# First pair's rotary steps on VectorE, and TensorE given turns and products ahead of the first scores, in a fused attention and gated feed-forward kernel

## The chip, the cores and the metric

The kernel runs on one core of a Trainium2 chip. The time is the device time of one execution, in microseconds (us). Of the kernel before, three runs are shown: 659.55 us in the median, 659.51 the lowest and 661.09 the highest. The engines are PE (TensorE, matmul), DVE (VectorE), ACT (ScalarE), POOL (GpSimd) and SP (SyncE, which issues most DMAs). Each works through its own list of instructions in order, and an instruction waits on semaphores for what other engines and DMAs have to finish first.

## The reference, cut to what matters

```
def rotate(x):                       # rotary position embedding, x: 8 x 8 heads x 576 x 64
    x1, x2 = (x[..., :half], x[..., half:])
    return np.concatenate([x1 * cos - x2 * sin, x1 * sin + x2 * cos], axis=-1)
scores = scale * np.matmul(rotate(q), rotate(k).transpose(0, 1, 3, 2))
attn = softmax(scores)               # max subtracted, exp, divided by the sum
x = np.matmul(attn, v)               # then heads side by side: 8 x 576 x 512
gate = sigmoid(causal 5-tap convolution of x along the positions, per channel)
out = ((gate * (x @ w_val)) @ w_out)
```

## The kernel before, in words

The 64 heads are worked off as 32 pairs, two heads on the 128 partitions. For each pair, q and k come in as [128, 2, 576]: the values, and the values with the two halves of the head swapped. The rotary step multiplies the first by the cosine table, the second by the sine table (`rope_mul`, L211, twice), adds them (`rope_add`, L215), rounds the sum to the fast matmul format on ACT (`qk_hi`, L222), and takes the rest of that rounding (`qk_lo`, L226). The scores are sums of three products of these high and low parts (`s_mm`, L254), in five chunks: four of 128 queries for both heads, c0 to c3, and a mixed one, c4, for the last 64 queries of both heads. A chunk of one head is a 576-wide tile in PSUM; there are three such buffers. DVE takes the row maximum (`s_max`, L260, called max0 to max8), ACT the exponential (`s_exp`, L273). The probabilities are turned on PE (`t_mm`, L302 and L315) or by DVE and DMAs (L288), multiplied with v (L358, L368, L373, L376), normed, convolved, and pass through the two weight matrices (L454).

One of the two heads reads its keys in a rotated order: its first 64 key columns are a copy of the last 64 (`k_front`, L189 on the tile k). So both heads' scores need the end of the keys first, and the copy needs the later key half.

The first pair's q and k come in two parts each, so that work can start early. Key halves are columns 0 to 287 and 288 to 575; the query parts are columns 0 to 255 and 256 to 575. The tables come in the same two halves on ACT's DMA queue, and ACT scales each (`scale_tab`, L207) before it is used. The keys of the plan end in `_0` and `_1` for the earlier and later part: `kmul0_0`, `kmul1_0`, `kadd_0`, `khi_0`, `klo_0` are the steps of the earlier key half.

The weight matrices w_val and w_out are stored as 64-bit floats. Each is loaded in four pieces of 512 KB and decoded on DVE and ACT in six steps, L488, L490, L491, L493, L494, L495, then split into a high and a low part with PE's help (L525 to L532). The decode of the first pieces of w_val stands between the first pair's maxima.

A planner sets the order: each step is a job with a due time, its base time plus an entry in the table `DUE`, and a list of tiles it reads, writes and holds. `Plan.order` takes the job with the earliest due time among those whose inputs are planned and whose buffers are free, and appends it to the list of its engine. `PICK` says on which engine a step runs (V for DVE, G for POOL). Buffers are counted: there is one buffer for a loaded q (`iq`), two for a loaded k (`ik`). So the load of the second pair's q can be planned only when every step of the first pair that reads iq is planned, and on the chip its DMA waits for the last of them. All loads but those of the tables stand on SP's list.

Of the kernel before, what the change touches and what calls it, by code (L numbers as in the profile page):

```python
# [28 lines left out]
G1 = 288  # L29
SCALE = 0.125  # L30
EARLY = 5
TURNED = {}
# [760 lines left out]
```

## Time and profile before

| | |
|---|---|
| median of 3 runs | 659.55 us |
| the profiled execution | 661.04 us, its span 658.9 us |
| busy in the span | PE 93%, DVE 88%, ACT 70%, POOL 60% |
| DVE's last step of the first pair's rotary work | ends at 13.46 us |
| first full chunk of scores | starts at 12.52 us |
| max0 | starts at 14.13 us |

The span is the time from the first to the last instruction, and all places in the program are given in us from its start. The busy shares are means over stages with different limits; the change lies in the first 30 us, so that stretch is read by itself. In a timeline, the bracket behind a row tells how long the engine had been idle and what ended it.

### The profile page before, as it was taken

How to read it: one execution, taken by the hardware profiler on the slowest of the kernel's cores; microseconds unless marked ns; L12 is line 12 of the kernel's file. 1: busy time of each engine (PE TensorE's matmuls, PEld its weight loads, DVE VectorE, ACT ScalarE, POOL GpSimd, SP SyncE). 2: the span in 40 equal slices, each digit the busy share in tenths (PEclk: the TensorE clock that was granted, in tenths of full speed). 3: DMA queues.
4: the chain of work that ended last, by engine and by line, in shares of the span. 5: the costliest groups of instructions: out<-in, count | busy, mean ns of one | idle time of the engine just before them, and what ended most of it. 6: DMA issues, size and time to landing. Idle time of an engine off the chain costs nothing.

```text
span 658.9 us, 15153 instructions
## 1 busy us (share of the span) xinstructions
PE 611.4 (93%) x5592; PEld 495.5 (75%) x5592; DVE 579.8 (88%) x830; ACT 459.5 (70%) x1152; POOL 397.0 (60%) x303
## 2 busy tenths in 40 slices
PE   1889888889989999999999999999999999999897
PEld 1666665578777887888788887888788877888696
DVE  5799988898899999999999999999999999984552
ACT  3677878677677677777787777777777777774421
POOL 2323346568577868687787768786967776630210
PEclk9999999899999999999999999999999999999999
DMA  7314432259999899899999999989999898774101
GB/s 276 123 57 143 142 128 98 96 153 264 267 246 265 232 260 244 224 277 236 267 247 256 248 272 255 264 236 264 240 260 265 221 265 248 200 178 116 38 27 63
DMA packets 51480, 134.40 MB, mean 204 GB/s; under 512 B 10928, under 2 KB 20944, under 8 KB 51408
## 3 DMA queue, kind: packets, MB, share of 16 engines
q1 hardware_dynamic: 50864, 132.86, 72.5%
q8 instruction: 44, 0.72, 0.5%
q10 hardware_dynamic: 544, 0.59, 0.3%
q14 instruction: 28, 0.23, 0.1%
HBM read 62.48 MB, written 9.59 MB: 109 GB/s over the span
## 4 chain that ended last, share of the span: by engine, by line
PE 75%; DVE 14%; ACT 5%; DMA 2%; issue 1%; SPq 1%; POOL 1%; DVEq 0%; ACTq 0%
PE ps_t L454 27%; PE ps_s L254 19%; PE ps_t L368 17%; DVE nm L260 4%; PE ps_t L358 3%; DVE big L288 2%; PE ps_t L373 2%; PE ps_t L329 2%; ACT p L273 2%; PE ps_t L302 2%; DVE g L428 1%; DMA ik<-in_k 1%; DVE big L191 1%; DMA big<-big 1%; SPq L293 1%
## 5 line engine op out<-in xcount | busy, mean ns | idle before, releaser
L273 ACT ACTIVATE p<-ps_s,nm 128x576 f32<-128x576 f32 x256 | 187.9, 738 | 78.9 <-DVE nm L260 77.8
L260 DVE TENSOR_REDUCE nm<-ps_s 128x1 f32<-128x576 f32 x288 | 202.1, 743 | 21.1 <-PE ps_s L254 20.5
L254 PE MATMUL ps_s<-k,q 64*128 64x288 f32 x1536 | 146.1, 314 | 20.8 <-ACT k L222 9.3
L254 PEld LDWEIGHTS ps_s<-k,q 64*128 64x128 f32 x1536 | 113.2, 188 | 44.7 <-issue 13.5
L288 DVE STREAM_TRANSPOSE big<-p 128x1152 f32<-128x1152 f32 x104 | 139.8, 1353 | 0.0
L428 DVE SCALAR_TENSOR_TENSOR g<-x,cw,g 128x576 f32<-128x576 f32 (+1 forms) x132 | 121.1, 917 | 2.1 <-ACT g L425 0.6
L368 PE MATMUL ps_t<-big,v 128*64 128x256 f32 (+2 forms) x1024 | 118.6, 384 | 0.0
L368 PEld LDWEIGHTS ps_t<-big,v 128*64 128x64 f32 x1024 | 70.9, 138 | 46.2 <-issue 15.1
L211 POOL TENSOR_TENSOR iq<-iq,tab 128x576 f32<-128x576 f32 (+1 forms) x59 | 84.3, 1443 | 29.7 <-DMA iq<-in_q 25.3
L215 POOL TENSOR_TENSOR ik<-ik 128x576 f32<-128x576 f32 x27 | 38.9, 1440 | 76.9 <-DVE ik L211 74.7
L454 PE MATMUL ps_t<-xh,wval_hi 128*128 128x288 f32 x256 | 78.3, 306 | 2.7 <-DVE g L459 2.0
L454 PE MATMUL ps_t<-yh,wout_hi 128*128 128x288 f32 x256 | 78.4, 306 | 1.1 <-ACT yh L463 1.1
L226 POOL TENSOR_TENSOR k<-ik,k 128x576 fp32r<-128x576 f32 x31 | 55.2, 1782 | 35.9 <-ACT k L222 34.8
L454 PE MATMUL ps_t<-yl,wout_hi 128*128 128x288 f32 x256 | 75.9, 296 | 0.1
L454 PE MATMUL ps_t<-xh,wval_lo 128*128 128x288 f32 x256 | 75.9, 297 | 0.0
L454 PE MATMUL ps_t<-yh,wout_lo 128*128 128x288 f32 x256 | 75.3, 294 | 0.0
L454 PE MATMUL ps_t<-xl,wval_hi 128*128 128x288 f32 x256 | 75.3, 294 | 0.0
L467 POOL TENSOR_TENSOR yl<-g,yh 128x288 fp32r<-128x288 f32 x56 | 45.8, 823 | 32.6 <-DVE g L428 25.2
L415 POOL TENSOR_TENSOR xl<-x,xh 128x576 fp32r<-128x576 f32 (+1 forms) x33 | 48.2, 1462 | 25.6 <-ACT xh L411 16.2
L226 POOL TENSOR_TENSOR q<-iq,q 128x576 fp32r<-128x576 f32 (+1 forms) x32 | 45.4, 1419 | 15.9 <-ACT q L222 15.8
L454 PEld LDWEIGHTS ps_t<-xh,wval_hi 128*128 128x128 f32 x256 | 48.1, 188 | 6.2 <-issue 2.6
L211 POOL TENSOR_TENSOR ik<-ik,tab 128x576 f32<-128x576 f32 (+1 forms) x32 | 45.5, 1421 | 11.5 <-DVE big L490 7.0
(91 smaller groups left out, 1072.2 us busy)
## 6 DMA issues: line engine op xcount, KB each, us to landing
big<-big SPq DMA_DIRECT2D x416, 144.0 KB
ik<-in_k SPq DMA_DIRECT2D x31, 576.0 KB
iq<-in_q SPq DMA_DIRECT2D x31, 576.0 KB
v<-in_v SPq DMA_DIRECT2D x32, 320.0 KB
rb<-rd SPq DMA_DIRECT2D x64, 144.0 KB
out_t<-oo SPq DMA_DIRECT2D x64, 144.0 KB
big<-in_w_val SPq DMA_DIRECT2D x4, 512.0 KB
big<-in_w_out SPq DMA_DIRECT2D x4, 512.0 KB
```

Source lines behind the costliest of these rows:

```text
L211: eng.tensor_tensor(out=t[:, i, a:b], in0=t[:, i, a:b], in1=tabs[:, i, a:b], op=ALU.mult)
L215: eng.tensor_tensor(out=t[:, 0], in0=t[:, 0], in1=t[:, 1], op=ALU.add)
L226: eng.tensor_tensor(out=t[:, 1], in0=state[p][n + "in"][:, 0, a:b], in1=t[:, 0].bitcast(F32), op=ALU.subtract)
L254: T.matmul(out=ps[:, half, 0:288], lhsT=st["q"][rows, x, c * 128:c * 128 + 128] if c < 4 else mixq[p % 2][:, x], rhs=st["k"][rows, y, k0:k ...
L260: V.tensor_reduce(out=st[f"nm{i}"], in_=st[f"s{i}"], axis=AX.XY, op=ALU.max, negate=True)
L273: A.activation(out=pd.rearrange("p (b x) -> p b x", b=2), in_=st[f"s{i}"], func=AF.Exp, bias=st[f"nm{i}"], scale=1.0, accum_out=sums[p % 2 ...
L288: V.transpose(out=t[:, :, cs.index(c)].rearrange("p b k i -> p k b i"), in_=st[f"p{c}"].rearrange("p h s -> p (h s)").rearrange("p (k b i) ...
L368: T.matmul(out=acc[HEAD[h], 0:n], lhsT=st["v"][:, j, h, :], rhs=st["pt"][:, :, c0:c1, 5 * place(p, 2 * c0 + h) + j].rearrange("p a c i -> ...
L415: eng.tensor_tensor(out=st["xl"][:, a:b], in0=xs[p % 2][:, 4 + a:4 + b], in1=st["xh"][:, a:b].bitcast(F32), op=ALU.subtract)
L428: V.scalar_tensor_tensor(out=g, in0=x_sb[:, a + k:b + k], scalar=w, in1=g, op0=ALU.mult, op1=ALU.add)
L454: T.matmul(out=acc[:, 0:n], lhsT=wt[w][:, kc, ds], rhs=mv, start=(kc == 0 and i == 0), stop=(kc == NCH - 1 and i == 2))
L467: eng.tensor_tensor(out=ffn[b, "l", dc, lo], in0=y, in1=ffn[b, "h", dc, lo].bitcast(F32), op=ALU.subtract)
```

## The change

Three things are altered. First, `PICK` sends `kmul1_0` and `qmul0_0` (one multiplication of the earlier key half and one of the first query part) from POOL to DVE, so that apart from the low part of the second query part the whole rotary work of the first pair stands on DVE. Second, the entries of `DUE` for the first pair's loads, table steps and rotary steps, and for the load of the taps, are set to values near -9900, so that they are planned ahead of everything else and in another order: the later half of the table first, and the later key half ahead of the earlier one. Third, a new function `warm` puts on PE 44 turns of the identity as its first instructions, and 8 products of the first query part with itself ahead of the first scores; nobody reads what they write.

```diff
 EARLY = 5
+WARM = (44, 8)
...
-DUE = { ... 'loadk_1': -2600.9, 'kmul0_1': -1714.63, 'loadq_0': -2599.1, 'qlo_1': -105.27, ... }
+DUE = { ... 'loadk_1': -9902.88, 'kmul0_1': -9882.88, 'loadq_0': -9880.1, 'qlo_1': -9707.36, ... }
-PICK = { ... 'kmul1_0': 'G', ... 'qmul0_0': 'G', ... }
+PICK = { ... 'kmul1_0': 'V', ... 'qmul0_0': 'V', ... }
...
+    def warm(k):
+        b = bank(f"ps_t/warm{k}")
+        for _ in range(WARM[k]):
+            if k:
+                T.matmul(out=b[:, 0:256], lhsT=parts["q"][0][:, 0, 0:128], rhs=parts["q"][0][:, 0, 0:256], start=True, stop=True)
+            else:
+                T.transpose(out=b[:, 0:128], in_=ident, identity=ident)
...
+    at("warm0", -20000, "PE", 8000, warm, 0, w="ps_t/warm0", mode="f")
     PERIOD = 18.5
     for p in range(NP):
...
+        if p == 0:
+            at("warm1", -150, "PE", 1000, warm, 1, r="q0#hi.0", w="ps_t/warm1", mode="f")
         at("kfront" + ph, t - 5, "A", {"A": (315, False), "V": (230, True)}, k_front, p, "ENGINE", pick="kfront" + ph, r=r, w=f"kf{par}")
```

Two places show what the planner makes of it. Behind them the lists of all engines read the same before and after.

The first is the start of SP's list, before. The numbers name buffers: iq0_157 is the second pair's q, in the one iq buffer, ik1_132 its k, ik0_205 the third pair's k, and big0 holds the first two pieces of w_val.

```order
L197 DMA ik0_102<-in_k2 128x2x288
L197 DMA iq0_104<-in_q2 128x2x256
L506 DMA oo0_106<-in_conv_w 128x40
L197 DMA ik0_102<-in_k2 128x2x288
L518 DMA big0_114<-in_w_val 128x1024
L197 DMA iq0_104<-in_q2 128x2x320
L518 DMA big0_114<-in_w_val 128x1024
L197 DMA ik1_132<-in_k2 128x1152
L518 DMA big1_137<-in_w_val 128x1024 x2
L197 DMA iq0_157<-in_q2 128x1152
L197 DMA ik0_205<-in_k2 128x1152
```

And now, where iq0_179 is the second pair's q, ik1_183 its k and ik0_259 the third pair's k:

```order
L198 DMA iq0_147<-in_q2 128x2x256
L198 DMA ik0_150<-in_k2 128x2x288
L515 DMA oo0_152<-in_conv_w 128x40
L198 DMA ik0_150<-in_k2 128x2x288
L198 DMA iq0_147<-in_q2 128x2x320
L198 DMA iq0_179<-in_q2 128x1152
L527 DMA big0_181<-in_w_val 128x1024
L198 DMA ik1_183<-in_k2 128x1152
L527 DMA big0_181<-in_w_val 128x1024
L527 DMA big1_186<-in_w_val 128x1024 x2
L198 DMA ik0_259<-in_k2 128x1152
```

The first query part leads, and the second pair's q has moved from the tenth place to the sixth, ahead of all four pieces of w_val and of the second pair's k; it waits, as before, for the last reader of the first pair's q.

The second place is DVE's list from the second of its rotary steps to max0, before (L211 is a multiplication, L215 the addition, L226 the low part, L488 the first decode step of w_val's first piece, L260 a maximum; ahead of these rows stands one multiplication of the earlier key half):

```order
L215 TENSOR_TENSOR ik0_102<-ik0_102 128x288
L211 TENSOR_TENSOR iq0_104<-iq0_104,tab_68 128x256
L215 TENSOR_TENSOR iq0_104<-iq0_104 128x256
L226 TENSOR_TENSOR q0_71<-iq0_104,q0_71 128x256
L226 TENSOR_TENSOR k0_69<-ik0_102,k0_69 128x288
L211 TENSOR_TENSOR ik0_102<-ik0_102,tab_68 128x288 x2
L215 TENSOR_TENSOR ik0_102<-ik0_102 128x288
L226 TENSOR_TENSOR k0_69<-ik0_102,k0_69 128x288
L211 TENSOR_TENSOR iq0_104<-iq0_104,tab_68 128x320 x2
L215 TENSOR_TENSOR iq0_104<-iq0_104 128x320
L488 TENSOR_SCALAR big0_114<-big0_114 128x512
L260 TENSOR_REDUCE nm0_161<-ps_s0_141 128x1
```

And now (L212, L216, L227, L497 and L261 are the same lines; ahead of these rows stand both multiplications of the first query part):

```order
L216 TENSOR_TENSOR iq0_147<-iq0_147 128x256
L227 TENSOR_TENSOR q0_71<-iq0_147,q0_71 128x256
L212 TENSOR_TENSOR ik0_150<-ik0_150,tab_68 128x288 x3
L216 TENSOR_TENSOR ik0_150<-ik0_150 128x288
L227 TENSOR_TENSOR k0_69<-ik0_150,k0_69 128x288
L212 TENSOR_TENSOR ik0_150<-ik0_150,tab_68 128x288
L216 TENSOR_TENSOR ik0_150<-ik0_150 128x288
L227 TENSOR_TENSOR k0_69<-ik0_150,k0_69 128x288
L212 TENSOR_TENSOR iq0_147<-iq0_147,tab_68 128x320 x2
L216 TENSOR_TENSOR iq0_147<-iq0_147 128x320
L497 TENSOR_SCALAR big0_181<-big0_181 128x512
L261 TENSOR_REDUCE nm0_215<-ps_s0_199 128x1
```

DVE has two multiplications more; of the three in a row on the keys, the first is the earlier half's, the other two the later half's. In both lists the first decode step of w_val (L488, now L497) stands directly ahead of max0. On ACT, the second half of the table is now scaled before the first rounding, and `k_front` has moved behind the rounding of the second query part.

## Rows read from the trace of the kernel before

**Rows 1.** The page's first part: busy time, share of the span, instructions.
```profile
PE 611.4 (93%) x5592; PEld 495.5 (75%) x5592; DVE 579.8 (88%) x830; ACT 459.5 (70%) x1152; POOL 397.0 (60%) x303
```
**Rows 2.** The chain that ended last, 0 to 62 us: start, length, engine, tile, line.
```profile
12.52 1.59 PE ps_s L254 x10
...
24.33 1.81 PE ps_s L254 x11
...
27.29 1.71 PE ps_t L532 x2
```
**Rows 3.** Timeline, 14 to 34 us, DVE: start, length, instruction, idle time before it.
```profile
17.41 0.76 DVE L260 TENSOR_REDUCE nm<-ps_s 128x1 f32<-128x576 f32 x1 [1.26 <-PE ps_s L254]
...
30.34 0.76 DVE L260 TENSOR_REDUCE nm<-ps_s 128x1 f32<-128x576 f32 x1 [2.50 <-PE ps_s L254]
```
**Rows 4.** Line L254 in 24.2 to 26.2 us and 31.8 to 33 us: shortest, median, longest ns.
```profile
L254 PE MATMUL ps_s<-k,q x11: 438/438/606, 24.3 to 25.7; 64*128 64x288 f32 x11
...
L254 PE MATMUL ps_s<-k,q x12: 287/291/397, 31.9 to 32.6; 64*128 64x288 f32 x12
```

**Rows 5.** Timeline, 4 to 15 us, the first pair's rotary work.
```profile
4.33 0.68 ACT L207 ACTIVATE tab<-tab 128x576 f32<-128x576 f32 x1 [1.33 <-DMA tab<-in_tab]
...
9.86 0.83 DVE L211 TENSOR_TENSOR ik<-ik,tab 128x288 f32<-128x288 f32 x2
...
11.21 0.43 ACT L222 CAST k<-ik 128x288 fp32r<-128x288 f32 x1 [1.39 <-DVE ik L215]
...
12.05 0.89 DVE L211 TENSOR_TENSOR iq<-iq,tab 128x320 f32<-128x320 f32 x2
12.17 0.30 ACT L189 CAST k<-k 128x128 fp32r<-128x128 f32 x1 [0.53 <-DVE k L226]
...
12.97 0.49 DVE L215 TENSOR_TENSOR iq<-iq 128x320 f32<-128x320 f32 x1
13.38 0.42 DVE L488 TENSOR_SCALAR big<-big 128x512 int32<-128x512 int32 x1
13.50 0.46 ACT L222 CAST q<-iq 128x320 fp32r<-128x320 f32 x1 [1.03 <-DVE iq L215]
...
14.04 0.86 POOL L226 TENSOR_TENSOR q<-iq,q 128x320 fp32r<-128x320 f32 x1 [6.03 <-ACT q L222]
14.13 0.76 DVE L260 TENSOR_REDUCE nm<-ps_s 128x1 f32<-128x576 f32 x1 [0.33 <-PE ps_s L254]
```
**Rows 6.** The tables' DMA queue, 5.2 to 5.4 and 5.4 to 5.6 us: packets, MB, share.
```profile
q10 hardware_dynamic: 5, 0.01, 8.0%
...
q10 hardware_dynamic: 1, 0.00, 0.3%
```
**Rows 7.** Timeline of SP's DMA issues, 0 to 60 us.
```profile
3.59 0.60 SPq L518 DMA_DIRECT2D big<-in_w_val  x1
...
14.93 0.33 SPq L197 DMA_DIRECT2D iq<-in_q  x1
15.30 0.43 SPq L197 DMA_DIRECT2D ik<-in_k  x1
```
**Rows 8.** SP's waits, 0 to 60 us: total, times, longest.
```profile
SPq L197 <- POOL q L226: 28.9, 3, 13.9
```
**Rows 9.** Timeline, the first use of the second pair's q.
```profile
18.95 1.75 POOL L211 TENSOR_TENSOR iq<-iq,tab 128x576 f32<-128x576 f32 x1 [2.20 <-DMA iq<-in_q]
```
**Rows 10.** DMA rate in 40 equal slices of 14 to 22 us.
```profile
GB/s 185 41 0 0 0 0 0 0 0 161 46 138 138 184 323 346 392 415 461 438 392 369 438 415 438 438 254 92 23 0 0 0 0 0 0 0 0 0 0 0
```
**Rows 11.** Timeline, 14 to 34 us, PE: four turns of a probability tile.
```profile
17.81 1.09 PE L302 MATMUL ps_t<-ident,p 128*128 128x128 f32 x4 [0.20 <-ACT p L273]
```
**Rows 12.** Windows: busy time of each engine, granted TensorE clock (PEclk), DMA share and rate.
```profile
119.00:120.00 1.00, 0.00 (x0) 0.00 (x0) 1.00 (x3) 0.00 (x0) 0.09 (x1) 1.00 0.51 118
...
121.00:122.00 1.00, 0.99 (x8) 0.29 (x4) 1.00 (x3) 0.43 (x2) 0.00 (x0) 0.53 0.00 0
...
124.00:125.00 1.00, 1.00 (x10) 0.55 (x8) 0.96 (x3) 0.50 (x3) 0.00 (x0) 0.77 0.00 0
```

More of the change, by code (lines that the diff above doesn't have):

```diff
@@ new lines @@
+DUE = {'vz': 23.6, 'vze': 15.3, 'taps': -9901, 'dtap': 21.24, 'ltab_0': -9870.0, 'stab_0': -9830.0, 'loadk_0': -9860.0, 'kmul0_0': -9780.0, 'kmul1_0': -9771.4, 'kadd_0': -9762.8, 'khi_0': -9754.2, 'klo_0': -9734.8, 'ltab_1': -9892.88, 'stab_1': -9842.88, 'loadk_1': -9902.88, 'kmul0_1': -9882.88, 'kmul1_1': -9874.28, 'kadd_1': -9865.68, 'khi_1': -9857.08, 'klo_1': -9817.68, 'loadq_0': -9880.1, 'qmul0_0': -9850.0, 'qmul1_0': -9841.4, 'qadd_0': -9832.8, 'qhi_0': -9814.2, 'qlo_0': -9804.8, 'loadq_1': -2599.7, 'qmul0_1': -9752.56, 'qmul1_1': -9733.96, 'qadd_1': -9725.36, 'qhi_1': -9716.76, 'qlo_1': -9707.36, 'kfronte': 9.51, 'qmixede': 12.23, 'loadve': 16.06, 's0e': -227.23, 'max0e': 13.73, 'exp0e': -339.41, 'max1e': 15.46, 'exp1e': -561.74, 's1e': -344.33, 'max2e': 12.59, 'exp2e': -68.28, 'max3e': 13.07, 'exp3e': -939.79, 's2e': 11.12, 'max4e': 14.21, 'exp4e': -768.86, 'max5e': 14.15, 'exp5e': -897.98, 's3e': -336.64, 'max6e': 15.22, 'exp6e': -1153.57, 'max7e': 15.22, 'exp7e': -160.89, 's4e': 11.95, 'max8e': 13.35, 'exp8e': 15.75, 't0e': 22.72, 'c0e': -119.34, 't1e': -192.14, 'c1e': 18.09, 't2e': -1447.45, 'c2e': -237.8, 't3e': 28.76, 'c3e': -1079.21, 't4e': 24.98, 'c4e': -326.1, 't5e': 21.07, 'c5e': 21.86, 't6e': -199.47, 'c6e': 16.33, 't7e': -188.93, 'c7e': 17.61, 'th1e': -932.6, 'ch1e': -424.79, 'th3e': -807.66, 'ch3e': 13.99, 'tme': 19.16, 'cme': -847.12, 'rinve': -2264.39, 'thme': -1195.39, 'chme': -1282.4, 'rwe': -825.13, 'rre': -20.58, 'xhie': -1613.61, 'xloe': -3315.12, 'tap0e': -58.62, 'tap1e': 14.84, 'tap2e': 26.14, 'tap3e': -35.71, 'tap4e': -280.96, 'gatee': -424.87, 'lval0': -744.78, 'dval0': -2.73, 'lval1': -329.96, 'dval1': 6.46, 'lval2': -212.92, 'dval2': -10.53, 'lval3': -161.36, 'dval3': -4.26, 'lout0': 33.92, 'dout0': 41.08, 'lout1': -38.15, 'dout1': -5.83, 'lout2': -42.59, 'dout2': 2.61, 'lout3': -9.02, 'dout3': 16.46, 'loadke': -522.91, 'kmul0e': 16.57, 'kmul1e': 10.33, 'kadde': 15.77, 'khie': -323.7, 'kloe': -335.33, 'loadqe': -1778.49, 'qmul0e': 15.87, 'qmul1e': 6.44, 'qadde': -530.8, 'qhie': -1386.96, 'qloe': -2011.52, 'f00': 39.37, 'f01': 38.45, 'f02': 36.05, 'f03': 33.98, 'f04': 14.16, 'f05': 57.36, 'f06': 50.07, 'f07': 20.21, 'f10': 29.06, 'f11': 17.31, 'f12': 20.92, 'f13': 20.77, 'f14': 40.92, 'f15': 43.76, 'f16': 25.69, 'f17': 38.33, 'loadk': -1078.23, 'kmul0': 0.53, 'kmul1': 16.98, 'kadd': -1350.24, 'khi': 18.76, 'klo': -1610.53, 'loadq': -384.18, 'qmul0': 3.26, 'qmul1': 5.91, 'qadd': -2018.7, 'qhi': 8.19, 'qlo': -1896.24, 'kfront': 17.8, 'qmixed': 16.62, 'loadv': 23.64, 's0': -615.54, 'max0': 17.71, 'exp0': -2901.14, 'max1': 16.98, 'exp1': -1877.53, 's1': 17.35, 'max2': -504.2, 'exp2': -4468.42, 'max3': -344.46, 'exp3': -2348.56, 's2': 17.89, 'max4': 17.43, 'exp4': -3148.82, 'max5': 17.12, 'exp5': -1548.82, 's3': 22.04, 'max6': -77.69, 'exp6': -1871.54, 'max7': 21.82, 'exp7': -2790.26, 's4': -339.41, 'max8': 22.7, 'exp8': -2605.32, 'x0': 15.55, 'x1': 19.39, 'x2': 21.03, 'x3': 20.75, 'x4': 24.67, 'x5': 23.33, 'x6': 20.54, 'x7': 21.88, 'tm': 26.37, 'cm': -884.96, 'rinv': 24.52, 'thm': -933.16, 'chm': -631.93, 'rw': -292.37, 'rr': 24.36, 'xhi': 31.16, 'xlo': -4576.9, 'tap0': -2383.93, 'tap1': 26.15, 'tap2': 28.12, 'tap3': 36.14, 'tap4': -411.6, 'gate': -891.23, 't0': -262.54, 'c0': -1691.36, 't1': 42.76, 'c1': -434.49, 't2': 25.32, 'c2': -1718.62, 't3': 53.27, 'c3': -1358.42, 't4': 39.43, 'c4': -1278.08, 't5': 34.66, 'c5': -3353.58, 't6': -89.01, 'c6': -675.93, 't7': -232.42, 'c7': -1808.92, 'th1': 22.4, 'ch1': -864.1, 'th3': 46.92, 'ch3': -1180.05, 'xhil0': -2099.68, 'xlol0': -375.24, 'tap0l0': -3628.89, 'tap1l0': -1727.91, 'tap2l0': -1835.19, 'tap3l0': 181.47, 'tap4l0': 25.55, 'gatel0': -1023.25, 'xhil1': -1503.17, 'xlol1': -696.91, 'tap0l1': 954.61, 'tap1l1': 2571.53, 'tap2l1': -1071.34, 'tap3l1': 218.81, 'tap4l1': -58.41, 'gatel1': 414.9, 'f0l0': 601.52, 'f0l1': 248.77, 'f0l2': 448.04, 'f0l3': 1347.11, 'f0l4': 3027.31, 'f0l5': 1209.45, 'f0l6': 1634.95, 'f0l7': 2882.08, 'f1l0': 2032.44, 'f1l1': 1849.05, 'f1l2': 2008.04, 'f1l3': 2721.13, 'f1l4': 736.1, 'f1l5': 2035.76, 'f1l6': 2263.47, 'f1l7': 2942.03, 'radd': -1399.39, 'radde': -3366.0, 'pv4': 26.64, 'pv0': -908.13, 'pv1': -175.08, 'norm0': 25.62, 'norm1': 24.65, 'pv4e': 18.34, 'pv0e': -1035.51, 'pv1e': -955.08, 'norm0e': -288.7, 'norm1e': -243.61, 'mv0': 26.57, 'mv1': -544.07, 'mv2': -117.24, 'mv3': -97.41, 'mv0e': 0.0, 'mv1e': 0.0, 'mv2e': 0.0, 'mv3e': 0.0}
```

3 lines of the change are left out of this document (1 added, 2 removed).

## The prediction

> **What bounds the kernel now.** The page is read first: PE is busy for 93% of the span, DVE for 88% [rows 1]. These are means over the whole run; the change lies in the first 30 us, so the second view is the chain that ended last, cut to that stretch. There it runs from the first loads through DVE's rotary steps into the scores on PE [rows 2], and on through DVE's maxima. Third, the timeline of DVE shows where it waits behind that: 1.26 us ahead of max2 and 2.50 us ahead of max8, both for scores [rows 3]. Nothing in the chain is tied to an absolute time except the first loads, and every list of instructions is fixed; so what moves max0 moves the rest by as much, less what these waits can give back.
>
> PE works at half rate there, though the page's line of granted clocks does not show it: the products of a chunk take 438 ns in the median at 24 us and 291 ns at 32 us [rows 4]. The chain's 1.59 us for c0 and 1.81 us for c3 [rows 2] are times at 1.2 GHz.
>
> **The rotary steps.** DVE's first multiplication now needs the first query part and the earlier half of the tables, which has become the second transfer on its queue. Before, the first transfer was there at 4.33 us [rows 5]; the second's packets run on to between 5.4 and 5.6 us [rows 6]. With landing at 5.7 and a scaling of 0.68 us [rows 5], DVE starts at about 6.4 us (bounds 5.8 to 6.7, by how the two queues share the engines now that SP's first transfer is 256 KB and not 288).
>
> From there DVE is one line of work, with a round trip to ACT in each part. The later key half shows it before: from 9.86 us to the next part's start at 12.05, 2.19 us for two multiplications, an addition, ACT's rounding (0.43 us, at 11.21) and the low part [rows 5]. The first query part is 256 columns of 288: 2.0 us, an estimate. The earlier half's first multiplication takes half of the 0.83 us that two take, 0.42; the later half 2.19; the remaining steps of the earlier half 2.19 - 0.42 = 1.77; the second query part to the end of its addition 12.05 to 13.46, 1.41 [rows 5]. Sum 7.8 us, so the addition ends at 14.2 us, before at 13.46 (12.97 + 0.49). The two multiplications taken from POOL therefore buy nothing: DVE does alone, later, what the two shared.
>
> Behind that addition stands ACT's rounding, 0.46 us, and now k_front behind it, 0.30 us [rows 5]: with 0.04 us per handover k_front is done at 15.05 us, and c0 starts at about 15.1 us instead of 12.52 [rows 2], 2.6 us later. This is not yet what sets the end.
>
> **SP's list.** The last reader of the first pair's q is POOL's low part of the second query part. Before, it starts 0.58 us behind the addition's end (13.46 to 14.04) and takes 0.86 us [rows 5]; at 14.93 us SP issues the second pair's q, directly behind it [rows 7]. That SP does stand there and hold what is behind it is seen twice: POOL's q ends three of its waits, 28.9 us in all [rows 8], and the k that follows is issued at 15.30 us [rows 7], though the last step on its buffer, the later key half's low part, was done at about 12.1 us. Now the addition ends at 14.2, POOL at 15.63, and the issue comes at about 15.7 us. Before, this held up nothing that was soon needed, since w_val's pieces had been issued from 3.59 us on [rows 7]. Now w_val's four pieces and the second pair's k stand behind it.
>
> How late does w_val's first piece land? The second pair's q takes 4.02 us, 14.93 to 18.95, by POOL's wait for it [rows 7, 9]. Together with the k behind it, 1152 KB, the packets are through at 19.8 us, the end of the last slice that moves anything [rows 10], 4.87 us after the first issue. Now it is 576 + 512 = 1088 KB. Below: those rates reach 1088 KB at 19.25 us, 4.3 us after the issue. Above: the piece comes as a whole behind the q, 4.02 plus 512 KB at the 0.42 MB per us of the full slices [rows 10], 5.3 us. I take 4.8, nearest to the pair that was measured: landing at 20.5 us.
>
> The wait that this adds is DVE's: the first decode step of that piece stands in its list directly ahead of max0, in both versions. Before it ran at 13.38 us without a wait [rows 5]. Now DVE stands still from 14.2 to 20.5 us; queued behind are max0, max1, the rest of the decode and all of DVE's work; ACT's exponentials wait for the maxima, PE's c1 for a PSUM buffer that the first exponential frees. With the decode step's 0.42 us and 0.05 us of handovers max0 starts at 20.95 us; before at 14.13 [rows 5]. That is 6.8 us. From the low ends (5.8 us start, 4.3 us landing) it is 5.7, from the high ones 7.6. POOL's work for the second pair begins once its k lands, 576 KB behind the piece, 1.4 us at that rate, at about 22 us. Before, POOL turned to that pair's q 4.8 us behind max0 (18.95 to 14.13) [rows 5, 9], now at 25.75; a step on the k of about 1.75 us, as on the q, has room for 2 us, so this is hidden.
>
> **Turns and products on PE.** The 44 turns have no input but the identity. Even if all run at half rate, at the 1.09 us that four turns take there [rows 11], they are 12.0 us and end by about 13.5; the 8 products, an estimate of 0.2 us each from c0's pace [rows 2], end by 15.1. So they don't delay c0, and a tenth or two would not matter. What they could give is c0 at full rate, 1.59 times 291/438 = 1.06 instead of 1.59 us [rows 2, 4]; but c0 is done by 16.9 us at either rate and max0 waits until 20.95, so this is worth nothing. Then PE has the first products of c1 and stops for its buffer until the first exponential is done, at 22.5 us (0.76 us of max0 and 0.74 of the exponential behind 20.95, with their handovers): more than 5 us without work. The trace shows what that does: with no PE work at 119 us the granted clock is 0.53 in the stretch from 121 us, next to the lower level of 1.2 GHz, and comes back to 2.4 GHz only within the stretch from 124 us, 0.77 [rows 12]. So c1 and what follows start at 1.2 GHz, as before, and I count no gain.
>
> The Trainium skill (TensorE: Matmul & The Clock Gate, in the part on HAM oscillation) warns of the same thing: a stretch without PE work, such as a wait for a DMA, puts the array back to half rate, whatever warmed it up ahead. By it the sum stays as it is; without it 2.0 us would go back, rival (1) below. The trace agrees with its clock of 0.53.
>
> **Sum.** 661.04 us for the profiled execution plus 6.8 gives 667.8. That execution is 1.49 us above the median of its kernel, and the drop of the clock at 121 us, which need not come in every run, lies in it; against the median, 659.55 + 6.8 = 666.35 us, and with a little given back at DVE's later waits 666.2.
>
> **Rivals.** (1) The clock does rise earlier: PE stays at 2.4 GHz, or gets there sooner in c1 to c3. Then c1, as long as c0, brings max2 forward by 1.59 - 1.06 = 0.53 us (of the 1.26), and c3 by the same ratio 0.61, with the weight products behind it (1.71 us for two, half of it saved at twice the clock, 0.85) shortens the 2.50 ahead of max8 by 1.46 [rows 2 to 4]. Together 2.0: 664.3 us. For it: PE is busy from the start. Against it: the gap, and rows 12.
>
> (2) Not slower: w_val's first piece is not what DVE waits for. If SP passed the second pair's q, or the piece landed by 15.6 us, max0 would follow c0: start 15.1, 1.06 us at full rate, max0 at 16.2 instead of 14.13, +2.1, and rival (1)'s 2.0 back: 659.6 us, no change. It decides at an issue of w_val before about 11 us. Against it: SP's wait ended at 14.93 in before with POOL's step, and that step comes later now.
>
> (3) Worse: the second pair's k lands so late that a second wait opens behind POOL. If it took 4.02 us behind the piece, as the q took by itself, it would land at 24.5, and POOL would reach the q 0.5 us late at 26.25; if w_val's second piece then shares the rate with it, up to 1.5 us: 667.7 us. Against it: the rate of rows 10 once transfers follow each other.
>
> **How the numbers follow.** The forecast 0.70, rival (1) 0.18, (2) 0.06, (3) 0.06. The forecast's own range is 665.2 to 667.3 by the bounds above; the range of 8 in 10 takes in most of rival (1): 663.2 to 668.0. A measurement of this kernel can tell 0.3%, 2.0 us, from no change. Faster than that 0.02, within it 0.05, slower 0.93, all of the last from the forecast and rivals (1) and (3).
>
> **What would show it.** In the changed profile: DVE's first multiplication at 5.8 to 6.7 us; SP's issue of the second pair's q at about 15.7 us with POOL's q as what ended its wait, and w_val's first piece right behind; a wait of DVE of about 6 us ahead of its first decode step, ended by the DMA of w_val; max0 at 20 to 21.7 us; products of c1 at about 438 ns each again; and from max0 on the same distances as before. A decode step without a wait, or w_val issued before 11 us, would prove the forecast wrong; products at 291 ns behind 22 us would make it rival (1).

## The result, and the profile after

The changed kernel is slower. It took 671.85 us in the median of 6 executions (666.89 to 674.76), the kernel before 661.37 in 6 beside it (659.51 to 668.78): a ratio of 1.0149, 95% interval 1.0113 to 1.0184, which is 7.5 to 12.2 us. Forecast were 666.2 us and at most 668.0. The profiled execution took 673.96 us, with a span of 670.2.

The page's busy times differ little from [rows 1]; PE's 9.4 us more are the turns, the products and slower matmuls:

```profile
PE 620.8 (93%) x5644; PEld 503.6 (75%) x5644; DVE 582.3 (87%) x832; ACT 460.1 (69%) x1152; POOL 395.2 (59%) x301
```

The loss begins in the chain that ended last. Of its first 60 us, these pieces (start, length, what) stand where [rows 2] had c0 at 12.52:

```profile
1.47 5.55 DMA tab<-in_tab
...
7.76 0.77 DVE iq L212 x2
...
15.09 0.50 DVE iq L216
...
16.16 0.88 POOL q L227
17.43 4.65 DMA big<-in_w_val
22.10 0.43 DVE big L497
```

PE is no longer in it up to 22 us: it goes from a table transfer through DVE's rotary steps and POOL's low part into the load of w_val. The timeline of the same stretch, with SP's issues among the rows (start, length, instruction, idle time before it and what ended it):

```profile
3.60 13.78 SPq L198 DMA_DIRECT2D iq<-in_q  x2
...
7.04 0.68 ACT L208 ACTIVATE tab<-tab 128x576 f32<-128x576 f32 x1 [2.10 <-DMA tab<-in_tab]
...
16.32 1.81 PE L255 MATMUL ps_s<-k,q 64*128 64x288 f32 x12 [1.91 <-ACT k L190]
...
17.43 0.43 SPq L527 DMA_DIRECT2D big<-in_w_val  x1
...
22.10 0.43 DVE L497 TENSOR_SCALAR big<-big 128x512 int32<-128x512 int32 x1 [6.52 <-DMA big<-in_w_val]
22.44 0.75 DVE L261 TENSOR_REDUCE nm<-ps_s 128x1 f32<-128x576 f32 x1
23.61 1.45 POOL L212 TENSOR_TENSOR ik<-ik,tab 128x576 f32<-128x576 f32 x1 [6.59 <-DMA ik<-in_k]
24.11 1.80 PE L255 MATMUL ps_s<-k,q 64*128 64x288 f32 x11 [5.98 <-ACT p L274]
25.02 1.41 POOL L212 TENSOR_TENSOR iq<-iq,tab 128x576 f32<-128x576 f32 x1
25.72 0.76 DVE L261 TENSOR_REDUCE nm<-ps_s 128x1 f32<-128x576 f32 x1 [1.26 <-PE ps_s L255]
...
32.40 1.05 PE L255 MATMUL ps_s<-k,q 64*128 64x288 f32 x11 [1.44 <-ACT p L274]
...
37.96 0.76 DVE L261 TENSOR_REDUCE nm<-ps_s 128x1 f32<-128x576 f32 x1 [2.06 <-PE ps_s L255]
```

The decode step that had run at 13.38 without a wait [rows 5] stands 6.52 us for w_val, whose first piece was issued at 17.43 instead of 3.59 [rows 7]. Max0 starts at 22.44, 8.31 us later than in [rows 5]; max2 still waits 1.26 us for c1 [rows 3], and max8 comes 7.62 us later than the 30.34 of [rows 3], since c3 ran at full rate in this execution (1.05 us against 1.81 [rows 2]). The last maximum of the program starts at 612.03 us, before at 600.72: 11.3 us later. So 7.6 us were lost by the first nine maxima, and 3.7 us somewhere behind them.

### The profile page after: what moved, and what is told of

The parts are those of the page before. It is cut to its first block, busy times and chain, and to the rows that moved or that the text cites. A ratio compares the mean times of both kernels' runs of the same rounds, so it can differ in the third digit from the quotient of the medians.

```text
span 670.2 us, 15253 instructions
## 1 busy us (share of the span) xinstructions
PE 620.8 (93%) x5644; PEld 503.6 (75%) x5644; DVE 582.3 (87%) x832; ACT 460.1 (69%) x1152; POOL 395.2 (59%) x301
## 4 chain that ended last, share of the span: by engine, by line
PE 60%; DVE 15%; DMA 10%; ACT 5%; SPq 5%; issue 2%; POOL 2%; ACTq 0%; DVEq 0%; POOLq 0%
PE ps_t L463 23%; PE ps_s L255 14%; PE ps_t L369 13%; DVE nm L261 4%; SPq L294 4%; DVE big L289 3%; DMA v<-in_v 3%; PE ps_t L359 2%; DMA big<-big 2%; DMA ik<-in_k 2%; PE ps_t L303 2%; PE ps_t L330 2%; ACT p L274 2%; PE ps_t L374 2%; DMA iq<-in_q 1%
## 5 line engine op out<-in xcount | busy, mean ns | idle before, releaser
L261 DVE TENSOR_REDUCE nm<-ps_s 128x1 f32<-128x576 f32 x288 | 202.0, 742 | 20.2 <-PE ps_s L255 19.5
L255 PE MATMUL ps_s<-k,q 64*128 64x288 f32 x1536 | 145.4, 313 | 19.2 <-ACT p L274 14.2
L369 PE MATMUL ps_t<-big,v 128*64 128x256 f32 (+2 forms) x1024 | 120.1, 388 | 0.0
L212 POOL TENSOR_TENSOR iq<-iq,tab 128x576 f32<-128x576 f32 x58 | 83.1, 1449 | 28.8 <-DMA iq<-in_q 26.1
L216 POOL TENSOR_TENSOR ik<-ik 128x576 f32<-128x576 f32 x27 | 38.9, 1441 | 75.3 <-DVE ik L212 75.3
L227 POOL TENSOR_TENSOR k<-ik,k 128x576 fp32r<-128x576 f32 x31 | 55.5, 1790 | 41.3 <-ACT k L223 37.9
L227 POOL TENSOR_TENSOR q<-iq,q 128x576 fp32r<-128x576 f32 (+1 forms) x32 | 45.5, 1422 | 24.7 <-ACT q L223 24.6
L212 POOL TENSOR_TENSOR ik<-ik,tab 128x576 f32<-128x576 f32 x31 | 44.2, 1427 | 13.1 <-DMA ik<-in_k 6.6
```

The lines of the kernel that those rows point to most:

```text
L212: eng.tensor_tensor(out=t[:, i, a:b], in0=t[:, i, a:b], in1=tabs[:, i, a:b], op=ALU.mult)
L216: eng.tensor_tensor(out=t[:, 0], in0=t[:, 0], in1=t[:, 1], op=ALU.add)
L227: eng.tensor_tensor(out=t[:, 1], in0=state[p][n + "in"][:, 0, a:b], in1=t[:, 0].bitcast(F32), op=ALU.subtract)
L255: T.matmul(out=ps[:, half, 0:288], lhsT=st["q"][rows, x, c * 128:c * 128 + 128] if c < 4 else mixq[p % 2][:, x], rhs=st["k"][rows, y, k0:k ...
L261: V.tensor_reduce(out=st[f"nm{i}"], in_=st[f"s{i}"], axis=AX.XY, op=ALU.max, negate=True)
L369: T.matmul(out=acc[HEAD[h], 0:n], lhsT=st["v"][:, j, h, :], rhs=st["pt"][:, :, c0:c1, 5 * place(p, 2 * c0 + h) + j].rearrange("p a c i -> ...
```

## The experiments

The theory is the prediction's: a load held on SP's list sets max0, and the rotary steps on DVE set when it is issued. Rivals: the turns and products on PE, TensorE's clock, and a late loss of the change's own. Each ratio is to runs of the kernel before beside it; the number of runs stands in brackets.

**The second pair's q behind w_val** (e1_weights_first). In the changed kernel only that load's place on SP's list is moved:

```diff
-at(f"load{n}{fx}", ... t - (24 if n == "k" else 19), "SP", ...
+at(f"load{n}{fx}", ... t - (24 if n == "k" else 19) + 1700 * (p == 1 and n == "q"), "SP", ...
```

> The changed kernel, but with the load of the second pair's q put behind w_val's four pieces in SP's list, as it was before. Theory S (SP's list): w_val's first piece is issued at about 4 us, DVE's first decode step no longer waits, and max0 follows c0, which starts at 16.3 us as in the changed kernel: max0 at about 18 us instead of 22.44, 3.8 us behind the kernel before (14.13). Time about 4 us over the kernel before, 4.4 us under the changed kernel. Theory R (the rotary line): what costs is the late table and the long line on VectorE, and the wait for w_val only lies over it: max0 would stay near 22 us and the time with it, 7 to 8 us over the kernel before.

Measured: 664.14 us in the median of 10 against 661.72 of 17; ratio 1.0046 (1.0015 to 1.0078). From its timeline:

```profile
4.25 0.60 SPq L527 DMA_DIRECT2D big<-in_w_val  x1
...
15.81 0.42 DVE L497 TENSOR_SCALAR big<-big 128x512 int32<-128x512 int32 x1
16.64 1.81 PE L255 MATMUL ps_s<-k,q 64*128 64x288 f32 x12 [1.91 <-ACT k L190]
...
18.25 0.76 DVE L261 TENSOR_REDUCE nm<-ps_s 128x1 f32<-128x576 f32 x1 [2.02 <-PE ps_s L255]
```

The decode step has no wait any more, and max0 waits for c0. So SP's list cost 22.44 - 18.25 = 4.2 us at max0, or 4.5 if the table half had been scaled at 7.04 us here too and not at 7.36. The 4.1 us that stay against [rows 5] are the later start of c0, 16.64 against 12.52 us, and belong to the rotary steps and the copy ahead of it; c0 itself took 1.81 us before as well. In the times, 1.0149 or 1.0101 (below) comes down to 1.0046.

**Without the turns and products** (e2_no_warm).

```diff
-at("warm0", -20000, "PE", 8000, warm, 0, w="ps_t/warm0", mode="f")
...
-at("warm1", -150, "PE", 1000, warm, 1, r="q0#hi.0", w="ps_t/warm1", mode="f")
```

> The changed kernel without the 44 turns and the 8 products. Theory S: max0 stays at 22.4 us, since it waits for w_val, and the time stays within 1 us of the changed kernel. Rival (the turns help): c0 or c1 to c3 become slower by the clock, and the time rises by 1 to 2 us. Second rival (the turns cost something, by the clock falling again later): it drops by about 1 us.

Measured: 669.11 us (4), ratio 1.0112 (1.0060 to 1.0164). From its timeline:

```profile
7.57 0.68 ACT L208 ACTIVATE tab<-tab 128x576 f32<-128x576 f32 x1 [2.75 <-DMA tab<-in_tab]
...
22.97 0.75 DVE L261 TENSOR_REDUCE nm<-ps_s 128x1 f32<-128x576 f32 x1
```

Max0 starts 15.40 us behind the scaling of the second table half; in the changed kernel 22.44 - 7.04 = 15.40 us too. What PE does ahead of c0 costs and gives nothing at max0. Behind max8 this can't be said: to the last maximum this profile takes 570.2 us, the three of the changed kernel 572.3 to 574.1, the kernel before 570.4 and 571.1. One execution of each, and a ratio known to half a per cent, don't tell whether the turns and products cost 2 us there.

**Only the waiting load, in the kernel before** (e3_before_weights_late). In the kernel before, w_val's pieces are planned behind the second pair's q, and nothing else is changed:

```diff
-DUE = { ... 'lval0': -744.78, ... 'lval1': -329.96, ... 'lval2': -212.92, ... 'lval3': -161.36, ... }
+DUE = { ... 'lval0': -0.45, ... 'lval1': -12.4, ... 'lval2': -24.35, ... 'lval3': -36.3, ... }
```

> The kernel before with one thing changed: in SP's list the second pair's q stands ahead of w_val's four pieces, as in the changed kernel; no rotary step is moved, no turns added. Theory S: SP waits for POOL's step until 14.93 us, w_val's first piece lands about 5.0 us later (as it did in the changed kernel: issue of the q at 17.05, landing at 22.07), DVE waits some 6 us ahead of its first decode step, max0 at about 20.3 us, 6.2 us late; time 5.5 to 6.2 us over the kernel before. Theory R: no rotary step is changed, so no change of time.

Measured: 669.43 us (4), ratio 1.0116 (1.0070 to 1.0163): without any of the other edits about as slow as the changed kernel, by 7.7 us (4.6 to 10.8) where 5.5 to 6.2 were expected. From its timeline:

```profile
15.23 0.33 SPq L197 DMA_DIRECT2D iq<-in_q  x1
15.61 2.07 SPq L518 DMA_DIRECT2D big<-in_w_val  x4
...
20.19 0.43 DVE L488 TENSOR_SCALAR big<-big 128x512 int32<-128x512 int32 x1 [6.42 <-DMA big<-in_w_val]
20.53 0.75 DVE L260 TENSOR_REDUCE nm<-ps_s 128x1 f32<-128x576 f32 x1
```

Max0 comes 6.4 us later than in [rows 5]. So the list alone costs 6.4 us, the rest of the change without it 4.1 (e1), and both together 8.3: the two overlap, since DVE's later line hides part of the wait.

**The earlier table half first again** (e4_table_first_half). In the changed kernel:

```diff
-DUE = { ... 'ltab_0': -9870.0, 'stab_0': -9830.0, ... 'ltab_1': -9892.88, 'stab_1': -9842.88, ... }
+DUE = { ... 'ltab_0': -9895.0, 'stab_0': -9845.0, ... 'ltab_1': -9880.0, 'stab_1': -9832.0, ... }
```

> The changed kernel with the two halves of the table loaded and scaled in the old order, the earlier half first; all else as changed. The second transfer of the table landed at 7.02 us in the changed kernel, where 5.7 was predicted. Theory S with that term: VectorE starts at 5.1 instead of 7.76 us, every step up to SP's issue moves forward by 2.6 us (issue at 14.4), w_val lands at 19.4, max0 at 19.8 us; time 2.6 us under the changed kernel, about 5 us over the kernel before. Rival: the later key half's steps then wait for the other half of the table, landing at about 7 us; since they come 3 us behind the first step, this should cost under 0.5 us.

Measured: 666.91 us (8), ratio 1.0069 (1.0031 to 1.0107). DVE's first multiplication starts at 4.92 us, since the half it needs is there first, and from its timeline:

```profile
14.69 0.43 SPq L527 DMA_DIRECT2D big<-in_w_val  x1
...
19.67 0.75 DVE L261 TENSOR_REDUCE nm<-ps_s 128x1 f32<-128x576 f32 x1
```

The issue comes 2.74 us earlier than in the first profile of the changed kernel, and so does max0 (2.77). Against its repetition below, whose table half landed early (issue at 15.99, max0 at 21.17), it is 1.3 and 1.5 us: about half of the 2.7 belongs to the late landing in that one profile.

**All three mended** (e5_all_three, e6_all_three_no_warm). The edits of e1 and e4, and ACT's rounding of the second query part planned behind the copy of the keys again. The first has 20 products instead of 8, the second neither turns nor products:

```diff
-DUE = { ... 'qhi_1': -9716.76, 'qlo_1': -9707.36, ... }
+DUE = { ... 'qhi_1': 32.69, 'qlo_1': -105.27, ... }
```

> The changed kernel with three places of the order mended: the earlier table half first, w_val's four pieces ahead of the second pair's q in SP's list, and k_front ahead of the rounding of the second query part on ACT; and 20 products instead of 8, so that PE is busy until the first scores. Theory S: VectorE starts at 5.0 us, k_front is done at 11.4, c0 starts at 11.4 and ends at 12.5 (if the clock is up), w_val's first piece is there; max0 is then held by VectorE's own line, which ends at 12.85, and comes behind one decode step at 13.2 us, 0.9 us ahead of the kernel before; with c0 and c1 at full rate up to 2 us more. Time 1 to 3 us under the kernel before. Theory R (the long line on VectorE costs in itself): max0 not ahead of 14.1 us, no gain.

> The same without any turns and products ahead of the scores. If the clock of c0 and c1 matters once max0 isn't held by a DMA, this is 0.5 to 2 us slower than with them; if the clock falls again in the gap ahead of c1 in both, the two agree within 0.5 us, and max0 comes at 13.2 to 13.4 us.

Measured: 659.52 us (12) with turns and products and 660.53 (12) without, against 661.24 of 34; ratios 0.9961 (0.9932 to 0.9991) and 0.9976 (0.9948 to 1.0004). From the timeline of the first:

```profile
11.20 1.56 PE L255 MATMUL ps_s<-k,q 64*128 64x288 f32 x13 [1.05 <-ACT k L223]
...
12.48 0.49 DVE L216 TENSOR_TENSOR iq<-iq 128x320 f32<-128x320 f32 x1
12.88 0.42 DVE L497 TENSOR_SCALAR big<-big 128x512 int32<-128x512 int32 x1
13.22 0.75 DVE L261 TENSOR_REDUCE nm<-ps_s 128x1 f32<-128x576 f32 x1
```

and of the second:

```profile
7.47 0.68 ACT L208 ACTIVATE tab<-tab 128x576 f32<-128x576 f32 x1 [2.65 <-DMA tab<-in_tab]
...
14.93 0.76 DVE L261 TENSOR_REDUCE nm<-ps_s 128x1 f32<-128x576 f32 x1
```

The first is slightly faster than the kernel before: its max0 comes 0.9 us before the 14.13 of [rows 5]. It has no wait at max0; DVE's own line of work bounds it, not c0. Both multiplications still stand on DVE here, so having them there does not cost by itself, against theory R. The place of the copy of the keys was not changed alone, so its share is open. The later max0 of the second, expected at 13.2 to 13.4, goes with its table half, scaled 1.70 us later than in the first (5.77 us). With turns and 20 products the first 13 products of the scores took 1.56 us, without them 2.30; but max0 waits for DVE in both, and the two times are the same within their intervals, so here too no gain from the turns is shown.

**No gap on PE ahead of c1** (e7_busy_gap). The changed kernel with 40 more unread products between c0 and c1:

```diff
-WARM = (44, 8)
+WARM = (44, 8, 40)
...
+if p == 0 and c == 0:
+    at("warm2", t + 3.6 * c + 0.1, "PE", 1000, warm, 2, r="q0#hi.0", w="ps_t/warm2 order", mode="f")
```

> The changed kernel with 40 more products that nobody reads, on PE between c0 and c1, where it was idle for 6 us; all else as changed. Rival (1) of the prediction sized: with PE busy up to c1 the clock should be at 2.4 GHz for c1 to c3 and the weight products; max0 stays at about 22.4 us, and max8, at 37.96 us in the changed kernel, comes up to 2 us earlier. If the clock isn't what the waits ahead of max2 and max8 hang on, nothing changes.

Measured: 665.71 us (10), ratio 1.0075 (1.0042 to 1.0109). From its timeline:

```profile
16.68 6.22 PE L439 MATMUL ps_t<-q 128*128 128x256 f32 x40
22.83 1.07 PE L255 MATMUL ps_s<-k,q 64*128 64x288 f32 x12
...
23.93 0.76 DVE L261 TENSOR_REDUCE nm<-ps_s 128x1 f32<-128x576 f32 x1 [0.88 <-PE ps_s L255]
...
30.34 1.80 PE L255 MATMUL ps_s<-k,q 64*128 64x288 f32 x11 [1.61 <-ACT p L274]
```

With PE kept busy c1 runs at full rate, 1.07 us instead of 1.80, and max2 waits 0.88 us instead of 1.26. But after shorter pauses of PE the clock falls again (0.81 in the window from 29 us, 0.50 in the next), c3 is slow, and from max0 (21.04, where 22.4 was expected, since the table half was scaled at 5.66) to max8 (37.09) it is 16.05 us, before 16.21. So rival (1) of the prediction, which counted 2.0 us back, needs both chunks fast. By the ratios the time is 1.7 us below that of e8_changed_again beside it, by the medians 2.7, with intervals that overlap.

**The changed kernel twice more, and the one before** (e8_changed_again, e10_changed_third, e9_before_again). No edit.

> The changed kernel once more. In its profile max0 to max8 were 8.3 to 7.6 us behind the kernel before, but the end 11.3 us: 1.4 us more were lost at about 130 us and 4.3 at about 487 us, 2.0 given back later. Theory: those are losses that come and go from run to run at the same program, by transfers and the clock, not by the change; then the front is again 7.6 us late to within 0.6, and what is lost behind it differs by more than 1 us from the first profile. Rival: they belong to the change; then they come again at the same places and size.

> The changed kernel a third time, to settle the size of the loss (1.0149 and 1.0101 so far) and how often the second table half lands late. Theory (the path: 6.9 to 8.3 us at the first maximum according to the landing of the second table half at 5.6 or 7.0 us, the rest variation): first maximum at 21.0 to 22.5, the offset of the ninth 7.5 to 7.8, ratio 1.010 to 1.013. Rival (the first result's size is the true one, a late loss of its own of 3 to 4 us): ratio 1.014 or more, and the jump of 4 us near 487 us again.

> The kernel before, unchanged, with a profile of its own. Question: is the part of the changed kernel's loss that comes late (in its first profile 3.7 us after the first decode, of them 4.3 us between 485 and 495 us) its own, or do two executions of one program differ by as much? Theory (variation): the first 120 us repeat within 0.3 us (first maximum at 14.0 to 14.2), and from there on jumps of 0.5 to 1.5 us at the same places as in the other profiles (near 133, 149, 214, 286, 323 and 554 us), either way, with an end 1 to 4 us from that of the first profile; ratio 1.000 within 0.004. Rival (the losses belong to the shifted program): the two profiles of before agree to the end within 0.5 us.

Measured: the changed kernel 668.37 us (9) against 661.24 (34), ratio 1.0101 (1.0068 to 1.0134); and 668.66 (6) against 661.57 (17), ratio 1.0100 (1.0074 to 1.0125). The kernel before against itself: 662.26 (10), ratio 0.9998 (0.9975 to 1.0021). From the timeline of the first repetition:

```profile
5.61 0.68 ACT L208 ACTIVATE tab<-tab 128x576 f32<-128x576 f32 x1 [0.83 <-DMA tab<-in_tab]
...
15.99 0.43 SPq L527 DMA_DIRECT2D big<-in_w_val  x1
...
20.83 0.43 DVE L497 TENSOR_SCALAR big<-big 128x512 int32<-128x512 int32 x1 [6.68 <-DMA big<-in_w_val]
21.17 0.75 DVE L261 TENSOR_REDUCE nm<-ps_s 128x1 f32<-128x576 f32 x1
...
38.10 0.76 DVE L261 TENSOR_REDUCE nm<-ps_s 128x1 f32<-128x576 f32 x1 [3.23 <-PE ps_s L255]
```

of the second:

```profile
6.17 0.69 ACT L208 ACTIVATE tab<-tab 128x576 f32<-128x576 f32 x1 [1.27 <-DMA tab<-in_tab]
...
21.69 0.75 DVE L261 TENSOR_REDUCE nm<-ps_s 128x1 f32<-128x576 f32 x1
```

and of the kernel before:

```profile
13.92 0.76 DVE L260 TENSOR_REDUCE nm<-ps_s 128x1 f32<-128x576 f32 x1 [0.33 <-PE ps_s L254]
...
30.68 0.76 DVE L260 TENSOR_REDUCE nm<-ps_s 128x1 f32<-128x576 f32 x1 [3.05 <-PE ps_s L254]
```

The first repetition is as expected: its max8 is 7.8 us late. The second meets its expectation at max0 and in the ratio but not at max8, which is 6.8 us late instead of 7.5 to 7.8, because c3 ran fast. The repetition of the kernel before bears out the variation from one execution to the next, if not to the letter: max0 at 13.92 instead of 14.0 to 14.2, max8 0.34 us later than in the first profile and the last maximum 1.0. From max0 to max8 the kernel before took 16.21 us once and 16.76 here, the changed one 15.52, 16.93 and 15.46: the rate at which c3 and the weight products run differs from one execution to the next. Behind that, in the first profile of the changed kernel, one place near 487 us alone held 4.3 of its 11.3 us: PE waited 2.6 us for a DMA and then ran on at the lower clock. The row of PE and the windows show it (in a window: its length, busy time of PE, its weight loads, DVE, ACT and POOL, granted clock, DMA share and rate; the first two windows are used further down):

```profile
487.02 1.29 PE L359 MATMUL ps_t<-big,v 64*64 64x256 f32 x8 [2.62 <-DMA ik<-in_k]
...
12.00:13.00 1.00, 0.00 (x0) 0.00 (x0) 0.97 (x3) 0.00 (x0) 0.00 (x0) 1.00 0.00 0
13.00:14.00 1.00, 0.19 (x1) 0.19 (x1) 0.50 (x2) 0.43 (x1) 0.00 (x0) 0.54 0.00 0
...
487.00:489.00 2.00, 1.98 (x12) 0.94 (x14) 1.96 (x2) 1.36 (x5) 1.92 (x2) 0.63 0.89 256
489.00:491.00 2.00, 2.00 (x12) 1.09 (x10) 1.30 (x2) 1.25 (x2) 0.63 (x2) 0.52 1.02 281
```

In both repetitions the clock is 1.00 from 485 to 491 us, and 0.7 and 1.4 us are lost around that place, in the second profile of before 0.1. A loss of 1.4 us near 133 us against the first profile of before, in all three profiles of the changed kernel, is in the second profile of before as well. The rival, a late loss of 3 to 4 us of the change's own, fell with these and with two ratios of 1.010. Open stays whether a smaller one is left: behind max8 the repetitions lost another 1.9 and 2.5 us to the last maximum (610.42 and 610.04 us), the second profile of before 0.7 (601.74), all against the first profile of before. The three profiled executions of the changed kernel took 1.7 to 3.9 us more than the medians of their runs, so their late losses need not stand for the medians. Nor is it explained why the first measurement lies above the other two (its interval overlaps with theirs), since one execution of each left a trace.

## Why the prediction was wrong in size and right in mechanism

The time lay 3.9 us above the upper end of the range. Every step is there, in its order. Three terms were too small: the landing of a table transfer, the base, and what comes behind max8, which was put at nothing.

**The rotary steps: this is the step that failed.** DVE was to start at 6.4 us, bounds 5.8 to 6.7, by a landing of the second table transfer at 5.7. It landed at 7.02 in the profiled execution, and DVE started at 7.76. The other terms held: the addition ended 7.8 us later as summed, 15.58. Six profiles have the same table transfers and the same loads of the first pair in the same order, the changed kernel's three and those of e1 (where w_val's pieces follow at once), e2 and e7; the scaling behind that transfer starts in them at 7.04, 5.61, 6.17, 7.36, 7.57 and 5.66 us. Where the load is also held on SP's list, max0 follows it by 15.40, 15.56, 15.52, 15.40 (e2) and 15.38 us (e7); the prediction's 20.95 - 5.7 is 15.25. So nearly all that is wrong at max0 is this one landing: 1.3 of 1.5 us in the first profile, none of 0.2 in the second. The prediction took its bounds from one execution of the kernel before, where the packets ended by 5.6 us [rows 6]; in the changed kernel the tables' queue still moved some between 6.4 and 6.8 us (packets, MB, share):

```profile
q10 hardware_dynamic: 2, 0.00, 0.9%
```

The packet records of all twelve profiles agree in the bulk: 95% of that queue's 544 packets were done by 4.9 to 5.2 us. What differs is the tail, whose last packet ended at 5.15 to 6.99 us, in the two profiles of the kernel before and in e3 at 5.45, 5.70 and 6.65. And where ACT was waiting, the scaling began 0.36 to 0.58 us behind the last packet, where the prediction allowed 0.1. Why a tail is long in one execution and short in another is not shown.

**SP's list.** Right. The issue of the second pair's q was forecast at 15.7 us and came at 17.05, 1.35 late, 1.3 of it by the term above; POOL's low part ended that wait. W_val's piece was usable 5.0 us later, at 22.1, against 4.8; the repetition has its issue at 15.99 and the decode step at 20.83, forecast 20.5. The 6.52 us wait of DVE is the forecast's "about 6 us". e1 and e3 show the mechanism from both sides.

**Turns and products on PE.** Right that they give nothing, for a reason that went further: the clock was down before c0. The turns were done at 8.75 us, sooner than the 13.5 reckoned at half rate, for they had sped up: 6 a us from 4 to 5 us, 11 from 7 to 8. The products ended at 10.69, and the next product, the first of the scores, came at 13.81. The granted clock is 1.00 in the window from 12 and 0.54 in the one from 13 us (above), and c0 took 1.81 us as if nothing had been there. c1's products at 1.80 us for 11 are the predicted half rate. The warning of the Trainium skill (TensorE: Matmul & The Clock Gate, HAM oscillation) that a gap undoes the warming is borne out by that 0.54 and by e7, where c1 without the gap took 1.07 us. But the length of the last gap alone does not settle it: in e1 the granted clock was already 0.75 in the window from 11 us, though PE's last product had ended at 11.00 there, with an earlier pause of 1.81 us ahead of the products.

**Sum.** The second small term is the base: 6.65 us were put on 659.55, the median of three executions. The kernel before had 661.37, 661.72, 661.24 and 661.57 in the four sets of runs, so the base was 1.7 to 2.2 us low; 661.5 + 6.65 is 668.15, beside 668.37 and 668.66 of the repetitions. Against those the loss was sized right (ratio times 661.5: 6.7 and 6.6 us). Against the first measurement 9.9 us, 3.2 more, stand beside 6.65. The third term is in its profile: 0.8 us more than forecast at max8 (7.62 to 6.8), but 3.7 us behind it, where the prediction had nothing, since "what moves max0 moves the rest by as much". The repetitions show 1.9 and 2.5 us there, two executions of the kernel before differ by 0.7, and how much of it is the change's own stays open. In the profiles of the repetitions the last maximum is 9.7 and 9.3 us late, more than the 6.6 us of the ratios; so the agreement of the sum with the ratios does not prove each of its terms.

**The rivals.** (2) fell with the wait of 6.52 us. (3) fell: POOL's step on the second pair's k started at 23.61 and the q followed at 25.02 without a wait. (1) came true in part and by chance: c3 ran fast in the first and third profiles and gave 0.7 us back, in the second it did not.

## What to carry to other kernels

When steps are moved, look at every load behind them on the issuing engine's list: a load that has to wait for a buffer holds all loads behind it, and at max0 it cost 4.2 us here, 6.4 in the kernel before, though the data held were not even for the same work. When an operand goes from the first transfer of a queue to the second, its landing must be bounded by the spread over several executions, not by one trace. A forecast of 1% needs a base from more than three executions, since medians of this kernel moved by 2 us and more (659.55 to 662.26).

## What the runs showed of the hardware that was not expected

The scaling of the second 288 KB of the tables, which starts when they land, began anywhere between 5.61 and 7.57 us in six executions with the same order of these loads, while that of the first 288 KB started at 4.01 to 4.25 us in all of them. Of the packets 95% were through by 5.2 us each time; the tail made the difference. And a warm clock can be lost ahead of the very work it was warmed for: PE had no work from 10.69 to 13.81 us, and the granted clock was 1.00 in the window from 12 us and 0.54 in the next; in e1 it fell to 0.75 in the window that began as the last product ended.
